# Weight buffers of two expert layers at six different starts modulo 256 bytes

## The chip, the cores and the metric

The kernel runs on one core of one Trainium2 chip. The metric is device time in microseconds of one execution, the median of several runs. Engine names are those of the profile: PE is TensorE (its weight loads are shown apart as PEld), DVE is VectorE, ACT is ScalarE, POOL is GpSimd, SP is SyncE, which here issues the DMAs.

## What is computed

Attention with a mixing matrix over the heads before and after the softmax, and behind it two expert layers (each an inner product into 2048 features, an activation and a product back to 768), all in float32:

```python
scores = scale * np.matmul(q, k.transpose(0, 1, 3, 2))        # q, k, v: (2, 12, 448, 64)
scores = np.einsum('bhij,hg->bgij', scores, w_pre)
attn = softmax over the last axis
attn = np.matmul(np.einsum('bhij,hg->bgij', attn, w_post), v)
x = attn as (896, 768)
h = x @ w_in;  x = (h * np.clip(h + 3, 0, 6) / 6) @ w_out     # w_in (768, 2048), w_out (2048, 768)
h = x @ w_in2; x = (max(h, 0) + alpha * min(h, 0)) @ w_out2
```

The weights w_in, w_out, w_in2 and w_out2 arrive as float64; the kernel makes float32 values of their bits itself.

## The kernel before, in words

**Attention, up to about 250 us.** Query rows are taken in tiles of up to 120 rows. Scores (`qk`, L192 to L200, the matmul at L197) are two matmuls per head, with qT as stationary and kT as moving operand. They are written to S, read back by `pull` (L204) so that ten rows of all twelve heads fill 120 partitions, mixed by `premix` (L220, matmul L224), put through the exponential, mixed again by `post` (L239, matmul L244, in which slices of e are stationary and wr is moving), and multiplied by v in `av` (L272, matmul L281).

**Experts.** A float32 product is made of three matmuls in the rounded type float32r, by `mm3` (L436 to L440, the matmul at L438): the high part of the weight with the high and the low part of the moving operand, then the low part of the weight with the high part of the moving operand. The stationary operand is 128 x 128 weights, 512 bytes per partition; the moving operand is 128 x 448, a whole tile of 1792 bytes per partition (xh and xl in the inner products, gh and gl in the products back). `in_layer` (L486) takes one weight block of 128 x 768 per feature block and makes 18 matmuls of it for each of the two batches; `out_layer` (L649) takes a weight block per pair of feature blocks and makes 36 of it in six accumulators. There are 64 blocks, 16 for each of the four weight matrices, and 36 matmuls for each.

**Weights.** Block i is loaded as 64-bit words (`load_w`, L332) and turned into a float32 in `wb` by `conv_magnitude` (ACT, L344), `conv_shift` and `conv_sign` (DVE, L352 and L361) and `conv_round` (POOL, L368). `conv_hi` (L373, the copy at L376) rounds it into `whi` on ACT, and `conv_lo` (L379, the subtraction at L382) puts the rest into `wlo` on POOL. In the loops this is done two blocks ahead of its use. `whi` and `wlo` have three buffers each, taken in turn, so that block i uses number i mod 3.

**Where the buffers lie.** `open_early` (L391) closes pools of the attention and opens the pool "w" in their place, on the right side of the memory, then a pool "gap" of 192 bytes (L398), then "x0" and "g0"; `open_x1` and `open_late` open the rest. The tiles of the pool "w" thus lie where kT, qT and the staging tiles of the attention lay, and their first writer waits for the last reader of those. Below, the *rest* of a tile is the remainder of its first byte's address, within a partition, by 256.

```python
hi = P["w"].tile([128, WC], R, tag="whi", bufs=3, name="whi")    # WC = 768, 3072 bytes
nc.scalar.copy(hi, b_t[i])
...
nc.tensor.matmul(p, wt[a], xt[c], start=(first and z == 0), stop=(last and z == 2))
```

Of the kernel before, what the change touches and what calls it, by code (L numbers as in the profile page):

```python
# [8 lines left out]
R = mybir.dt.float32r  # L9
# [26 lines left out]
def kernel(  # L36
# [29 lines left out]
    for b in range(B):  # L66
        for i0 in range(0, S, GP):
            n = min(GP, S - i0)
            t = len(tiles)
# [31 lines left out]
    with tc.manual_schedule():  # L101
# [201 lines left out]
        for ti in range(1, NTILE):  # L303
            lo, hi = tiles[ti - 1]["s"] - PL, tiles[ti]["s"] - PL
# [5 lines left out]
        for ti in range(NTILE - 1):  # L310
            lo = tiles[ti]["s"] + tiles[ti]["ng"] + LAG
# [4 lines left out]
        P = {}  # L316
        WC = w_in1.shape[2]
# [50 lines left out]
        def conv_round(i):  # L368
            if i < len(blocks):
                n = b_t[i].bitcast(I32)  # L370
                nc.gpsimd.tensor_tensor(n, n, st_t.pop(i)[:, :, 0].bitcast(I32), ALU.add)  # L371

        def conv_hi(i):  # L373
            if i < len(blocks):
                hi = P["w"].tile([128, WC], R, tag="whi", bufs=3, name="whi")
                nc.scalar.copy(hi, b_t[i])  # L376
                w_t[i] = [hi]

        def conv_lo(i):  # L379
            if i < len(blocks):  # L380
                lo = P["w"].tile([128, WC], R, tag="wlo", bufs=3, name="wlo")
                nc.gpsimd.tensor_tensor(lo, b_t.pop(i), w_t[i][0].bitcast(F32), ALU.subtract)  # L382
                m = KD if blocks[i][0] == "in" else 2
                w_t[i] = [x.rearrange("p (k f) -> p k f", k=m) for x in (w_t[i][0], lo)]
# [101 lines left out]
        def in_layer(i, xs, act, gs, f0):  # L486
            for f in range(f0, KF):
                conv_round(i + 2)
                load_w(i + 4)
                conv_magnitude(i + 3)  # L490
                for c in range(B):
                    p = in_chain(i, xs, c)
                    gs[f, c] = g_tile(f, c)
                    a = act(p, gs[f, c], f)
                    next(a)
                    if c == 0:
                        conv_shift(i + 3)
                        next(a)
                        conv_hi(i + 2)
                        conv_lo(i + 2)  # L500
                    else:
                        conv_sign(i + 3)
                        next(a)
                    run(a)
                w_t.pop(i)
                i += 1
            return i
# [46 lines left out]
        for i in range(NC):  # L554
            at(X + 2 + 3 * i, lambda i=i: conv_hi(i), lambda i=i: conv_lo(i))
# [78 lines left out]
        for f in range(NC):  # L634
            p = in_chain(f, x_t, 1)
            w_t.pop(f)
            if f + 3 < 5:
                conv_hi(f + 3)
                conv_lo(f + 3)
            gs[f, 1] = g_tile(f, 1)  # L640
            run(act1(p, gs[f, 1], f))
            if f + 3 < 5:
                load_w(f + 5)
                if f == 0:
                    conv_round(4)
                else:
                    conv_a(5)
# [117 lines left out]
```

## Time and profile before

| | |
|---|---|
| median of 3 runs | 710.85 us (710.15 to 712.19) |
| span of the profiled execution (the page gives no time beside it) | 710.7 us |
| PE busy, PEld busy | 693.8 us (98%), 608.7 us (86%) |
| DVE, ACT, POOL busy | 414.7, 376.5, 335.3 us |
| granted PE clock | 1.000 over the span |
| matmul records of the expert layers (L438) | six groups of 384, each 138.5 to 141.9 us busy |
| subtraction of the low part (L382), 64 times | 132.3 us, mean 2067 ns |
| copy of the high part (L376), 64 times | 53.1 us, mean 830 ns |

A matmul's own duration counts from its start to its modelled end, and matmuls overlap, so the durations of a group add up to more than the time it fills; the distance between the starts of two matmuls tells how fast they follow each other. The same holds for the weight loads, which overlap the matmul before.

### The profile page before, as it was taken

The numbers are of one execution on the slowest core, as the hardware profiler recorded it, in microseconds if no ns is written. First come the engines' busy times: TensorE is split into PE (matmuls) and PEld (weight loads), VectorE is DVE, ScalarE is ACT, GpSimd is POOL, SyncE is SP. The second block draws the span as 40 slices with busy tenths as digits, with TensorE's granted clock in tenths as the row PEclk, the third lists the DMA queues.
The fourth block names the chain that finished last, engine by engine and source line by source line (L and its number), as shares of the span: only waits on it lengthen the run. The fifth ranks groups of instructions, "written<-read, shape, count | busy, mean of one in ns | idle before, by whom it ended". The sixth has DMA issues, their size and how long they took to land.

```text
span 710.7 us, 11175 instructions
## 1 busy us (share of the span) xinstructions
PE 693.8 (98%) x4164; PEld 608.7 (86%) x4164; DVE 414.7 (58%) x790; ACT 376.5 (53%) x704; POOL 335.3 (47%) x224
## 2 busy tenths in 40 slices
PE   5899999999999999999999999999999999999998
PEld 3577777877788879998889999999999999999997
DVE  5565486456666557777774354437777778335311
ACT  4576566657776646656654453344454545433310
POOL 6331175212225244656667755444555556664630
PEclk9999999999999999999999999999999999999999
DMA  4853554346445023233234424331323243424302
GB/s 127 231 187 109 190 162 125 116 141 185 158 110 165 1 71 109 90 98 124 89 100 155 146 89 134 102 121 52 127 92 131 90 132 102 157 98 169 131 1 77
DMA packets 31875, 85.21 MB, mean 120 GB/s; under 512 B 5966, under 2 KB 21966, under 8 KB 31822
## 3 DMA queue, kind: packets, MB, share of 16 engines
q1 hardware_dynamic: 31822, 84.50, 36.6%
q8 instruction: 33, 0.54, 0.3%
q14 instruction: 20, 0.16, 0.1%
HBM read 62.47 MB, written 2.75 MB: 92 GB/s over the span
## 4 chain that ended last, share of the span: by engine, by line
PE 77%; issue 9%; POOL 7%; DVE 2%; DMA 2%; ACT 2%; SPq 1%; POOLq 0%; ACTq 0%
PE p L438 49%; PE pt L244 9%; PE mx L224 9%; PE av L281 5%; POOL wb L371 4%; PE sc L197 4%; POOL wlo L382 2%; PE sc L186 1%; DMA pull<-S 1%; DMA kst<-in_k_dram 0%; DVE nm L226 0%; DVE xl L295 0%; ACT xh L294 0%; DMA qst<-in_q_dram 0%; DVE wr L218 0%
## 5 line engine op out<-in xcount | busy, mean ns | idle before, releaser
L382 POOL TENSOR_TENSOR wlo<-wb,whi 128x768 fp32r<-128x768 f32 x64 | 132.3, 2067 | 164.7 <-ACT whi L376 164.7
L371 POOL TENSOR_TENSOR wb<-wb,wst 128x768 int32<-128x768 int32 x64 | 130.5, 2040 | 57.7 <-DVE wb L364 37.6
L438 PE MATMUL p<-xh,whi 128*128 128x448 f32 x384 | 141.9, 370 | 1.1 <-ACT xh L294 1.1
L438 PE MATMUL p<-xh,wlo 128*128 128x448 f32 x384 | 139.2, 362 | 0.6
L438 PE MATMUL p<-xl,whi 128*128 128x448 f32 x384 | 139.7, 364 | 0.0
L438 PE MATMUL p<-gl,whi 128*128 128x448 f32 x384 | 139.4, 363 | 0.0
L438 PE MATMUL p<-gh,whi 128*128 128x448 f32 x384 | 139.2, 362 | 0.0
L438 PE MATMUL p<-gh,wlo 128*128 128x448 f32 x384 | 138.5, 361 | 0.3
L356 DVE TENSOR_SCALAR wb<-wb 128x768 f32<-128x768 f32 x64 | 62.1, 970 | 90.9 <-ACT wb L348 90.9
L348 ACT ACTIVATE wb<-wst 128x768 f32<-128x768 f32 x64 | 58.1, 908 | 77.0 <-DMA wst<-in_w_out_dram 46.5
L244 PEld LDWEIGHTS pt<-wr,e 120*112 120x112 f32 x720 | 86.8, 176 | 7.5 <-issue 2.3
L234 ACT ACTIVATE e<-mx,nm 120x448 f32<-120x448 f32 (+1 forms) x90 | 57.4, 637 | 62.6 <-DVE sm L215 45.3
L244 PE MATMUL pt<-wr,e 120*112 120x120 f32 x720 | 88.5, 266 | 0.0
L224 PE MATMUL mx<-pull,wmix_pre 120*120 120x448 f32 x180 | 84.1, 549 | 3.5 <-DMA pull<-S 3.2
L226 DVE TENSOR_REDUCE nm<-mx 120x1 f32<-120x448 f32 (+1 forms) x90 | 56.0, 622 | 47.0 <-PE mx L224 47.0
L438 PEld LDWEIGHTS p<-xh,whi 128*128 128x128 f32 x384 | 72.0, 188 | 9.0 <-ACT xh L294 2.8
L438 PEld LDWEIGHTS p<-xh,wlo 128*128 128x128 f32 x384 | 71.9, 187 | 7.2 <-POOL wlo L382 2.5
L438 PEld LDWEIGHTS p<-xl,whi 128*128 128x128 f32 x384 | 72.1, 188 | 5.8 <-issue 1.1
L438 PEld LDWEIGHTS p<-gh,wlo 128*128 128x128 f32 x384 | 71.8, 187 | 6.0 <-POOL wlo L382 1.0
L438 PEld LDWEIGHTS p<-gh,whi 128*128 128x128 f32 x384 | 72.1, 188 | 5.6
L376 ACT CAST whi<-wb 128x768 fp32r<-128x768 f32 x64 | 53.1, 830 | 43.2 <-PE p L438 39.1
L197 PE MATMUL sc<-kT,qT 128*120 128x448 f32 (+1 forms) x168 | 73.8, 524 | 2.0 <-POOL kT L154 0.9
(52 smaller groups left out, 863.3 us busy)
## 6 DMA issues: line engine op xcount, KB each, us to landing
wst<-in_w_in_dram SPq DMA_DIRECT2D x32, 768.0 KB
wst<-in_w_out_dram SPq DMA_DIRECT2D x32, 768.0 KB
pull<-S SPq DMA_DIRECT2D x88, 210.0 KB
qst<-in_q_dram SPq DMA_DIRECT2D x20, 180.0 KB
kst<-in_k_dram SPq DMA_DIRECT2D x5, 672.0 KB
v<-in_v_dram SPq DMA_DIRECT2D x8, 336.0 KB
out_dram<-o SPq DMA_DIRECT2D x12, 224.0 KB
qst<-in_q_dram SPq DMA_DIRECT2D x8, 132.0 KB
```

Source lines behind the costliest of these rows:

```text
L197: nc.tensor.matmul(p[:n, :S], t[:, o, a:a + n], kT[h], start=(o == 0), stop=(o == 1))
L224: nc.tensor.matmul(m[:pn, :S], wpre[:pn, :pn], d[:pn], start=True, stop=True)
L226: nc.vector.tensor_reduce(nm[:pn], m[:pn, :S], axis=AX.X, op=ALU.max, negate=True)
L234: nc.scalar.activation(out=e[:pn], in_=m[:pn, :S], func=ACTF.Exp, bias=nm[:pn], accum_out=sm[:pn])
L244: nc.tensor.matmul(p[:, c * GP:(c + 1) * GP], e[:pn, c * JP:(c + 1) * JP], wr[:pn], start=True, stop=True,)
L281: nc.tensor.matmul(p[64 * o:64 * o + 64, a % 3, :n], v_t[T["b"], h // HC][:, h % HC, c, :], MT[ti][:, c, h, :n], start=(c == 0), stop=(c = ...
L348: nc.scalar.activation(t, s[:, :, 1].bitcast(F32), ACTF.Abs)
L356: nc.vector.tensor_scalar(t, t, W_MAX, W_MIN, ALU.min, ALU.max)
L371: nc.gpsimd.tensor_tensor(n, n, st_t.pop(i)[:, :, 0].bitcast(I32), ALU.add)
L376: nc.scalar.copy(hi, b_t[i])
L382: nc.gpsimd.tensor_tensor(lo, b_t.pop(i), w_t[i][0].bitcast(F32), ALU.subtract)
L438: nc.tensor.matmul(p, wt[a], xt[c], start=(first and z == 0), stop=(last and z == 2))
```

## The change

The pool "w" gets six tags with one buffer each in place of two tags with three. Each buffer is a little longer than the block (784 elements, the last 816), and the block starts 0, 4, 8 or 12 elements (0 to 48 bytes) into it. The starts are all multiples of 16 bytes. The six buffers together take 18944 bytes in place of 18432, 512 more, so that every tile that lies behind them keeps its rest.

```diff
@@ -370,15 +370,21 @@
                 n = b_t[i].bitcast(I32)
                 nc.gpsimd.tensor_tensor(n, n, st_t.pop(i)[:, :, 0].bitcast(I32), ALU.add)
 
+        def part(i, tag, more, starts):
+            z = i % 3
+            room = WC + 16 + (more if z == 2 else 0)
+            t = P["w"].tile([128, room], R, tag=f"{tag}{z}", bufs=1, name=tag)
+            return t[:, starts[z]:starts[z] + WC]
+
         def conv_hi(i):
             if i < len(blocks):
-                hi = P["w"].tile([128, WC], R, tag="whi", bufs=3, name="whi")
+                hi = part(i, "whi", 0, (0, 4, 8))
                 nc.scalar.copy(hi, b_t[i])
                 w_t[i] = [hi]
 
         def conv_lo(i):
             if i < len(blocks):
-                lo = P["w"].tile([128, WC], R, tag="wlo", bufs=3, name="wlo")
+                lo = part(i, "wlo", 32, (0, 0, 12))
                 nc.gpsimd.tensor_tensor(lo, b_t.pop(i), w_t[i][0].bitcast(F32), ALU.subtract)
                 m = KD if blocks[i][0] == "in" else 2
                 w_t[i] = [x.rearrange("p (k f) -> p k f", k=m) for x in (w_t[i][0], lo)]
```

In the built programs the blocks start at these rests:

| block number i mod 3 | whi before | whi now | wlo before | wlo now |
|---|---|---|---|---|
| 0 | 192 | 192 | 192 | 0 |
| 1 | 192 | 80 | 192 | 128 |
| 2 | 192 | 224 | 192 | 48 |

Slices of 128 columns lie 512 bytes apart, so a slice has its block's rest. The moving operands xh, xl, gh and gl start at rest 0 before and now. In the attention, which does not change, the stationary tiles start at other rests: the mixing matrix of L224 at 0; the four slices of e, 448 bytes apart, at 0, 192, 128 and 64; the slices of qT at all multiples of 32; v at 160, 96 and 224.

No engine's instructions change their order. The waits of four instructions on POOL do, since the buffers now lie over other old tiles. This is POOL's order at the first three low parts, before (xl is the splitting of x, wb and wst belong to the conversion):

```order
L382 TENSOR_TENSOR wlo<-wb,whi 128x768 [waits PE_49,Activation_49]
L434 TENSOR_TENSOR xl<-xT,xh 128x448 [waits Activation_49] x2
L434 TENSOR_TENSOR xl<-xT,xh 128x448 [waits DVE_49,Activation_49,Pool_49]
L382 TENSOR_TENSOR wlo<-wb,whi 128x768 [waits PE_49,Activation_49]
L434 TENSOR_TENSOR xl<-xT,xh 128x448 [waits Activation_49]
L382 TENSOR_TENSOR wlo<-wb,whi 128x768 [waits Activation_49]
```

and now:

```order
L388 TENSOR_TENSOR wlo<-wb,whi 128x768 [waits Activation_49]
L440 TENSOR_TENSOR xl<-xT,xh 128x448 [waits Activation_49] x2
L440 TENSOR_TENSOR xl<-xT,xh 128x448 [waits DVE_49,Activation_49,Pool_49]
L388 TENSOR_TENSOR wlo<-wb,whi 128x768 [waits Activation_49]
L440 TENSOR_TENSOR xl<-xT,xh 128x448 [waits Activation_49]
L388 TENSOR_TENSOR wlo<-wb,whi 128x768 [waits PE_49,Activation_49]
```

The first two subtractions no longer wait for PE, the third does. A little later stands the rounding of block 3, before:

```order
L434 TENSOR_TENSOR xl<-xT,xh 128x240 [waits DMAHW3_49,DMAHW4_49,DMAHW2_49,DMAHW5_49,DMAHW1_49,DMAHW6_49,DMAHW0_49,Activation_49]
L434 TENSOR_TENSOR xl<-xT,xh 128x240 [waits Activation_49] x4
L371 TENSOR_TENSOR wb<-wb,wst 128x768 [waits DMAHW6_49,DVE_49]
L434 TENSOR_TENSOR xl<-xT,xh 128x240 [waits Activation_49]
L382 TENSOR_TENSOR wlo<-wb,whi 128x768 [waits PE_49,Activation_49,Pool_49]
```

and now:

```order
L440 TENSOR_TENSOR xl<-xT,xh 128x240 [waits DMAHW3_49,DMAHW4_49,DMAHW2_49,DMAHW5_49,DMAHW1_49,DMAHW6_49,DMAHW0_49,Activation_49]
L440 TENSOR_TENSOR xl<-xT,xh 128x240 [waits Activation_49] x4
L371 TENSOR_TENSOR wb<-wb,wst 128x768 [waits DMAHW6_49,DVE_49,PE_49]
L440 TENSOR_TENSOR xl<-xT,xh 128x240 [waits Activation_49]
L388 TENSOR_TENSOR wlo<-wb,whi 128x768 [waits PE_49,Activation_49,Pool_49]
```

The rounding has a wait for PE more. In all of these the PE instruction waited for is a score matmul of the attention (L197).

## Rows read from the trace of the kernel before

**Rows 1.** the page: span, busy times by engine (share of the span, instructions)

```profile
span 710.7 us, 11175 instructions
...
PE 693.8 (98%) x4164; PEld 608.7 (86%) x4164; DVE 414.7 (58%) x790; ACT 376.5 (53%) x704; POOL 335.3 (47%) x224
```

**Rows 2.** the chain of waits in order of time, from 369 us: start us, us, what

```profile
369.03 338.29 PE p L438 x1690
```

**Rows 3.** windows of L438 alone: stretch, length, busy us by engine (instructions), clock, DMA

```profile
369.00:708.00 339.00, 338.27 (x1690) 316.80 (x1690) 1.00 0.32 110
```

**Rows 4.** L197, scores: ns smallest/median/largest, first and last start us

```profile
L197 PE MATMUL sc<-kT,qT x168: 358/369/722, 15.1 to 204.4; 128*120 128x448 f32 x120, 128*88 128x448 f32 x48
```

**Rows 5.** first low parts on GpSimd, timeline: start us, us, engine, line, operation

```profile
213.67 1.82 POOL L382 TENSOR_TENSOR wlo<-wb,whi 128x768 fp32r<-128x768 f32 x1
```

**Rows 6.** weight loads by line and shape: count | busy us, mean ns | idle before

```profile
L244 PEld LDWEIGHTS pt<-wr,e 120*112 120x112 f32 x704 | 84.9, 176 | 7.4 <-issue 2.3 <-ACT xh L433 0.4 <-ACT MT L257 0.2
L438 PEld LDWEIGHTS p<-xl,whi 128*128 128x128 f32 x384 | 72.1, 188 | 5.8 <-issue 1.1
...
L281 PEld LDWEIGHTS av<-MT,v 112*64 112x64 f32 x768 | 36.9, 137 | 2.1 <-ACT t L458 0.3 <-issue 0.3
L224 PEld LDWEIGHTS mx<-pull,wmix_pre 120*120 120x120 f32 x176 | 25.5, 183 | 6.3 <-POOL qT L169 2.9 <-issue 1.6 <-ACT e L234 1.3
L197 PEld LDWEIGHTS sc<-kT,qT 128*120 128x120 f32 x120 | 21.5, 183 | 25.1 <-issue 18.0 <-POOL qT L170 2.3 <-POOL kT L154 1.7
L197 PEld LDWEIGHTS sc<-kT,qT 128*88 128x88 f32 x48 | 7.6, 158 | 9.9 <-issue 9.1 <-POOL qT L170 0.4 <-POOL qT L169 0.2
```

**Rows 7.** L438 over the whole run: ns smallest/median/largest, starts

```profile
L438 PEld LDWEIGHTS p<-xl,whi x384: 186/188/192, 220.0 to 591.3; 128*128 128x128 f32 x192
```

**Rows 8.** timeline of the steady rhythm

```profile
600.15 0.36 PE L438 MATMUL p<-gh,wlo 128*128 128x448 f32 x1
...
600.34 0.36 PE L438 MATMUL p<-gh,whi 128*128 128x448 f32 x1
600.35 0.19 PEld L438 LDWEIGHTS p<-gl,whi 128*128 128x128 f32 x1
600.55 0.36 PE L438 MATMUL p<-gl,whi 128*128 128x448 f32 x1
```

**Rows 9.** timeline with loads that start late

```profile
255.23 0.36 PE L438 MATMUL p<-xh,wlo 128*128 128x448 f32 x1
...
255.25 0.19 PEld L438 LDWEIGHTS p<-xh,whi 128*128 128x128 f32 x1
255.43 0.37 PE L438 MATMUL p<-xh,whi 128*128 128x448 f32 x1
...
255.51 0.19 PEld L438 LDWEIGHTS p<-xl,whi 128*128 128x128 f32 x1
255.63 0.37 PE L438 MATMUL p<-xl,whi 128*128 128x448 f32 x1
```

**Rows 10.** L438 from 540 to 700 us

```profile
L438 PE MATMUL p<-gl,whi x180: 363/363/363, 592.1 to 699.5; 128*128 128x448 f32 x180
...
L438 PE MATMUL p<-gh,wlo x180: 360/360/360, 592.3 to 699.7; 128*128 128x448 f32 x180
```

**Rows 11.** L438 from 275 to 320 us

```profile
L438 PE MATMUL p<-xh,whi x76: 360/360/363, 274.7 to 319.7; 128*128 128x448 f32 x76
...
L438 PE MATMUL p<-xh,wlo x75: 360/363/363, 275.1 to 319.5; 128*128 128x448 f32 x75
```

**Rows 12.** tile whi: the instructions that write it, and that make wlo from it

```profile
L376 ACT CAST whi<-wb x64: 816/832/858, 212.4 to 685.6; 128x768 fp32r<-128x768 f32 x64
L382 POOL TENSOR_TENSOR wlo<-wb,whi x64: 1817/1885/2567, 213.7 to 686.5; 128x768 fp32r<-128x768 f32 x64
```

**Rows 13.** windows, all engines: stretch, length, busy us PE, PEld, DVE, ACT, POOL

```profile
540.00:700.00 160.00, 160.00 (x802) 150.00 (x801) 80.85 (x111) 60.76 (x81) 84.51 (x43) 1.00 0.32 108
```

**Rows 14.** L438 from 323 to 370 us: what ended its idle time

```profile
  POOL wlo L382: 3.5, 7
```

## The prediction

> **What bounds the kernel.** I read the page first, then the chain of waits, then the groups, timelines and windows of the expert matmuls (L438). The page is to show TensorE busy for 98% of a span of 710.7 us [rows 1]. The chain is to show what that work is in the second half: from 369.03 us to within 4 us of the end it is one piece, 338.29 us of L438 [rows 2]. Over those last 340 us nothing but the distance from one matmul to the next sets the time. No separate time stands beside the span of the profiled execution; the runs' median of 710.85 us is 0.15 above the span, and I carry the forecast on the runs' scale.
>
> The distance itself comes from the windows: 1690 matmuls in 338.27 us of busy time [rows 3], 200.2 ns each, at a granted clock of 1.00, which is the 2.4 GHz level. 448 columns at 2.4 GHz are 186.7 ns (an estimate), so 13.5 ns of each matmul is something else. There are 2304 such matmuls (64 blocks of 36), so 31.0 us of the run is at stake, and 1 ns per matmul is 2304 ns, 0.32% of the time. About 0.3%, 2.1 us, is also what a measurement of this kernel can tell from no change. The question is therefore narrow: does a weight buffer's start move the distance by 0.9 ns or more?
>
> **The change, part by part.**
>
> *Instructions.* None is added, removed or moved. The three buffers of each tag rotated by i mod 3 before and do so now. Price 0.
>
> *Waits.* Because the weight pool is 512 bytes longer, its buffers lie over other tiles of the attention. Two of GpSimd's first three low-part subtractions lose a wait for TensorE; the third, and the rounding of block 3, gain one. These are waits for readers of the old kT and qT tiles, and the last score matmul starts by 204.4 us [rows 4], while the first low part is computed from 213.7 us on [rows 5]. Old and new waits are over before they are reached, so I count 0 for both. If I read that wrongly, what is queued behind the waiting subtraction is GpSimd's splitting of x, and behind that TensorE's first expert matmuls.
>
> *Weight loads.* Five of the six buffers that the 2304 loads read start elsewhere. At rest 192 they take 188 ns [rows 6]. No row shows 128 columns at another rest, so the nearest rows must do: loads of 64 columns average 137 ns, of 88 columns 158, of 112 columns 176, of 120 columns 183 (the scores and the first mix alike), of 128 columns 188 [rows 6]. From 64 to 128 columns that is 51 ns over 64 columns, 0.8 ns a column; the line gives 156, 175 and 182 in between, and the rows lie within 2 ns of it. These loads start at very different rests: the mixing matrix at 0, e at 0, 192, 128 and 64 (slices of 448 bytes), qT at all multiples of 32 (three buffers, slices of 480 bytes). The number of columns explains the load; little is left over for the start. So I take 0. The ends come from the spread of the 128-column loads, 186 to 192 ns against 188 [rows 7]: 2 ns less or 4 ns more. If the distance followed the load one for one, that would be 2304 x 2 ns = 4.6 us less, or 2304 x 4 ns = 9.2 us more.
>
> Does the distance follow the load? In the steady rhythm a load starts within 0.01 us of the previous matmul, and the matmuls lie at 600.15, 600.34 and 600.55 [rows 8]. At 255.51 us a load starts 0.08 us after its predecessor's matmul at 255.43, and its own matmul still starts 0.20 us after that one, at 255.63 [rows 9]. A load started 0.07 us late costs nothing, so a load longer by a few ns should cost nothing either. The same rows speak to a clash of the two reads. A load at another moment of the stream meets other bytes of the moving operand, just as a load from another rest does, and the loads that start 0.02 and 0.08 us into the stream leave 0.20 us.
>
> *The moving operand.* Its tiles shift by 512 bytes or not at all, and keep rest 0. Price 0.
>
> *A trace of an address effect?* Matmuls with the low parts last 360 ns, those with the high weights and gl 363 [rows 10]. But from 275 to 320 us the 360 ns belongs to the high weights with xh, and the low weights have a median of 363 [rows 11], with the same buffers and rests. The 3 ns belong to a rhythm of three matmuls, not to a buffer.
>
> *Other engines.* ScalarE writes the high part in 816 to 858 ns, GpSimd the low part in 1.8 to 2.6 us [rows 12]. In the steady stretch neither disturbs TensorE: from 540 to 700 us, with ScalarE busy for 60.76 of 160 us and GpSimd for 84.51 [rows 13], every gl matmul takes 363 ns and every gh matmul with a low part 360, smallest as largest [rows 10]. Only from 323 to 370 us does TensorE wait for the low part, 3.5 us in 7 waits [rows 14]. If the new rests shortened GpSimd's work, at most these 3.5 us would go; lengthening each of 7 by 70 ns, the difference between smallest and median low part [rows 12], adds 0.5 us. I take 0.
>
> **A rule against the rows.** The row gives 200.2 ns a matmul. The Trainium skill, "TensorE: Matmul & The Clock Gate", section "Back-to-back issue gap", gives a gap of columns / 2.4 GHz + 2.5 ns, an estimate of 189.2 ns here, so the row disagrees by 11 ns; were this the new rests' doing to mend, the sum would be 710.9 - 25.3 = 685.6 us. The Trainium skill, "SBUF — State Buffer", section "Who interferes with whom", speaks against any effect of this change: TensorE never waits for anyone at the memory; by that the sum stays as it is, and the 13.5 ns are something that placing cannot touch.
>
> **Sum.** 0 + 0 + 0 + 0: 710.9 us.
>
> **The rivals.**
>
> *Faster: the 13.5 ns are collisions of the weight read with the moving read, and equal rests of all six buffers made the worst of it.* For it: the excess is there in every matmul, and all loads have one and the same relation (192 against 0), so the trace cannot show a better one. Against it: the late loads [rows 9] and the line through the load times [rows 6]. Price: if the two thirds of matmuls with high parts fell from 363 to the 360 ns of the best slot [rows 10], 1536 x 3 ns = 4.6 us, which gives 706.3 us. The far end is the whole excess, 31.0 us, 680 us; I see no row that supports more than a fraction of it, and a third of it would be 700.5.
>
> *Slower: some of the new rests are worse than 192.* Mechanism: one low buffer now starts at rest 0, on the moving operand's own rest, and two others (80 and 48) at odd multiples of 16 bytes; loads from these take longer or hold up the stream, and the distance follows. Place: every matmul from 369 us on, where nothing else covers it. Price: the largest load seen, 4 ns above the median [rows 7], on all 2304 is 9.2 us, 720.1 us; on half of them 4.6 us, 715.5 us. It decides from a mean of 0.9 ns per matmul. For it: 192 is the only rest whose distance is known, and a mean over six others can fall to either side. Against it: the same two sets of rows.
>
> *The change does nothing because the start is not what the reads see.* That is the forecast itself in its strictest form: same distance, 710.9 us.
>
> **How the numbers follow.** No change worth measuring, with all terms at 0: 0.48; the late loads and the load times speak for it, both from matmuls that are not exactly these. Faster: 0.28, since the excess of 31 us leaves much room and I know of no row that says what it is. Slower: 0.24, since the price per ns is the same, but there is less that a load can lose before it covers the distance. The range goes down to 703.0, beyond the 706.3 of the faster rival but short of a third of the excess, and up to 718.0, between half and all of the slower rival's 9.2 us. Outside I leave about 0.1 on either side. The likeliest case's own range is 708.8 to 713.0.
>
> **What would show it.** If I am right, the windows from 369 us on again give 200.2 ns per matmul, loads stay at 186 to 190 ns and the chain again ends in one piece of about 338 us. If the faster rival holds, the distance falls in that window, and the matmul groups with whi and wlo show shorter durations or split into values by buffer; if the slower one, the loads' median or largest grows and the 1690 matmuls take longer than 340 us. A changed distance in the window where all else is equal makes the forecast wrong; a change only before 369 us would mean that a wait or GpSimd's work did it.

## The result and the profile after

The changed kernel takes 716.12 us (median of 4 runs, 715.37 to 718.22) beside 710.89 us (710.15 to 712.19) for the kernel before: a ratio of 1.0071, 95% interval 1.0058 to 1.0083. That is slower by 5.2 us, where the forecast was no change; the time is within the range given and near the slower rival's 715.5. The traced execution of the changed kernel is the longest of its four, 718.22 us.

The page of the changed kernel, span and TensorE, which answer to [rows 1]:

```profile
span 716.4 us, 11174 instructions
...
PE 699.8 (98%) x4164; PEld 609.1 (85%) x4164; DVE 414.1 (58%) x790; ACT 376.0 (52%) x704; POOL 336.4 (47%) x224
```

The chain of waits in order of time (start, length, what), which answers to [rows 2]; the matmul's line is L444 now:

```profile
370.27 342.75 PE p L444 x1690
```

The chain reaches its last piece 1.2 us later than before (370.27 against 369.03), and the same number of matmuls, 1690, takes 4.5 us longer. Of the 1.2 us, 1.0 stands already at the first expert matmul (at 220.66 us against 219.69), before TensorE has read any of the moved buffers; in the other runs below that matmul starts between 217.4 and 219.9 us, so this part is no price of the rests. The loss is in the distance between matmuls. The windows of L444 from 369 us on, as in [rows 3] (stretch, length, busy us of PE and PEld, clock, DMA share, GB/s):

```profile
369.00:708.00 339.00, 338.97 (x1674) 313.88 (x1673) 1.00 0.32 107
```

338.97 us by 1674 is 202.5 ns a matmul in place of 200.2, at the same granted clock of 1.00. The groups of L444 from 540 to 700 us, as in [rows 10] (ns smallest/median/largest):

```profile
L444 PEld LDWEIGHTS p<-gh,whi x172: 187/188/188, 595.9 to 699.9; 128*128 128x128 f32 x172
L444 PE MATMUL p<-gh,whi x171: 362/365/369, 596.0 to 699.5; 128*128 128x448 f32 x171
...
L444 PE MATMUL p<-gl,whi x171: 362/363/370, 596.3 to 699.7; 128*128 128x448 f32 x171
L444 PEld LDWEIGHTS p<-gh,wlo x171: 187/188/189, 596.3 to 699.7; 128*128 128x128 f32 x171
L444 PE MATMUL p<-gh,wlo x171: 360/363/369, 596.5 to 699.9; 128*128 128x448 f32 x171
```

The weight loads are as long as before, 187 to 189 ns. The matmuls, which all had one value per group, now spread up to 369 and 370 ns. The next view is the timeline of the matmuls that begin four successive blocks of 36 (start, length):

```profile
377.18 0.37 PE L444 MATMUL p<-gh,whi 128*128 128x448 f32 x1
...
384.54 0.36 PE L444 MATMUL p<-gh,whi 128*128 128x448 f32 x1
...
391.83 0.37 PE L444 MATMUL p<-gh,whi 128*128 128x448 f32 x1
...
399.07 0.37 PE L444 MATMUL p<-gh,whi 128*128 128x448 f32 x1
```

and two successive ones of the kernel before:

```profile
390.35 0.36 PE L438 MATMUL p<-gh,whi 128*128 128x448 f32 x1
...
397.55 0.36 PE L438 MATMUL p<-gh,whi 128*128 128x448 f32 x1
```

Before, every block takes 7.20 us. Now the one with its parts at 192 and 0 takes 7.36, that at 80 and 128 takes 7.29, that at 224 and 48 takes 7.24, and so they repeat to the end. The three together lose 0.29 us; over 64 blocks that would be 6.1 us (an estimate). Some of that is given back early on, where TensorE waited for GpSimd's low part: the waits for it from 323 to 370 us are 1.8 us, 4 times, in place of 3.5 us, 7 times [rows 14]:

```profile
  POOL wlo L388: 1.8, 4
```

The slowest block has its high part where it always was, at rest 192, and yet from 377.18 us on all three of its products lie 203 to 206 ns apart, those with the high part too. So the rest of the buffer that a load reads does not by itself set the price of its own matmul. Three theories were put to the chip: A, what counts is how the rest changes from one load to the next; B, what counts is a weight's rest against that of the moving operand; C, what counts is the change from block to block. B later got two forms: R, the *distance* (the weight's rest less the moving operand's, modulo 256) decides, and S, the weight's own start does.

### The profile page after: what moved, and what is told of

Read it like the earlier page. It is cut to its first block, busy times and chain, and to the rows that moved or that the text cites. A ratio compares the mean times of both kernels' runs of the same rounds, so it can differ in the third digit from the quotient of the medians.

```text
span 716.4 us, 11174 instructions
## 1 busy us (share of the span) xinstructions
PE 699.8 (98%) x4164; PEld 609.1 (85%) x4164; DVE 414.1 (58%) x790; ACT 376.0 (52%) x704; POOL 336.4 (47%) x224
## 4 chain that ended last, share of the span: by engine, by line
PE 77%; issue 9%; POOL 6%; DMA 2%; DVE 2%; ACT 2%; SPq 1%; POOLq 0%; ACTq 0%
PE p L444 50%; PE pt L244 9%; PE mx L224 8%; PE av L281 5%; POOL wb L371 4%; PE sc L197 4%; POOL wlo L388 2%; DMA pull<-S 1%; PE sc L186 1%; DMA qst<-in_q_dram 1%; DMA kst<-in_k_dram 1%; DVE nm L226 0%; DVE xl L295 0%; ACT xh L294 0%; SPq L208 0%
## 5 line engine op out<-in xcount | busy, mean ns | idle before, releaser
L444 PE MATMUL p<-xh,whi 128*128 128x448 f32 x384 | 143.1, 373 | 1.1 <-ACT xh L294 1.1
L444 PE MATMUL p<-gh,whi 128*128 128x448 f32 x384 | 140.3, 365 | 0.0
L444 PE MATMUL p<-xh,wlo 128*128 128x448 f32 x384 | 140.0, 365 | 0.2
L444 PE MATMUL p<-xl,whi 128*128 128x448 f32 x384 | 140.2, 365 | 0.0
L444 PE MATMUL p<-gh,wlo 128*128 128x448 f32 x384 | 140.0, 364 | 0.2
L444 PE MATMUL p<-gl,whi 128*128 128x448 f32 x384 | 139.9, 364 | 0.0
L224 PE MATMUL mx<-pull,wmix_pre 120*120 120x448 f32 x180 | 84.0, 549 | 3.9 <-DMA pull<-S 3.2
L444 PEld LDWEIGHTS p<-xh,whi 128*128 128x128 f32 x384 | 72.0, 188 | 9.4 <-ACT xh L294 2.8
L444 PEld LDWEIGHTS p<-xl,whi 128*128 128x128 f32 x384 | 72.2, 188 | 6.9 <-issue 1.1
L444 PEld LDWEIGHTS p<-xh,wlo 128*128 128x128 f32 x384 | 72.2, 188 | 6.8 <-POOL wlo L388 1.3
L444 PEld LDWEIGHTS p<-gh,wlo 128*128 128x128 f32 x384 | 72.2, 188 | 6.6 <-POOL wlo L388 0.9
L444 PEld LDWEIGHTS p<-gl,whi 128*128 128x128 f32 x384 | 72.2, 188 | 5.6
L444 PEld LDWEIGHTS p<-gh,whi 128*128 128x128 f32 x384 | 72.0, 188 | 5.8
```

Of the source, the lines that this page charges most:

```text
L224: nc.tensor.matmul(m[:pn, :S], wpre[:pn, :pn], d[:pn], start=True, stop=True)
```

## The experiments

All experiments share one layout: six tags with buffers of 832 elements (13 times 256 bytes), so that a starting element sets the rest of each block freely, and every other tile keeps its rest unless said otherwise. The first one in full:

```diff
+        def part(i, tag, starts):
+            t = P["w"].tile([128, WC + 64], R, tag=f"{tag}{i % 3}", bufs=1, name=tag)
+            return t[:, starts[i % 3]:starts[i % 3] + WC]
...
-                hi = P["w"].tile([128, WC], R, tag="whi", bufs=3, name="whi")
+                hi = part(i, "whi", (16, 16, 16))
...
-                lo = P["w"].tile([128, WC], R, tag="wlo", bufs=3, name="wlo")
+                lo = part(i, "wlo", (16, 16, 16))
```

Below, a *triple* is the sum of three successive distances between matmul starts in the trace, for the three products of one slice; means leave out the first three triples of a block and those with a wait in them. Before, every steady triple from 380 us on is 600 ns.

**The rests undone, the rest of the change kept.** All six at 192, with starts (0, 0, 0):

> The six tags with longer buffers as in the change, the pool 1536 bytes longer than before, but all six blocks at rest 192 again: the rests undone, all the rest of the change kept. If the rests are the whole of it (theory R): 200.2 ns per matmul, no change against the kernel before, 711 us, and no run near 716. If the tags, the places or the moved waits have a share in the 5 us: 712 to 716 us.

Measured: 711.37 us (10 runs, 710.70 to 712.31) against 711.53 of the kernel before beside it, ratio 0.9999 (0.9989 to 1.0009). Windows from 369 us:

```profile
369.00:708.00 339.00, 337.70 (x1689) 316.19 (x1687) 1.00 0.33 110
```

200 ns per matmul (337.70 / 1689), and every steady triple is 600 ns. Six tags, longer buffers and other places cost nothing measurable in this layout, and the rests are what is left to explain the 5.2 us. (The pool is 1536 bytes longer than before here, in the change 512, so the change's own places and moved waits were not run by themselves.)

**All at rest 0**, starts (16, 16, 16) for both parts:

> All six weight buffers at rest 0, the moving operand's own rest, each block 0 and equal. Theory A (what counts is how far the rest changes from one load to the next): no change of rest anywhere, so 200.2 ns per matmul and 710.9 us, as before. Theory B (what counts is a buffer's rest against the moving operand's): rest 0 is the bad one, since block number 0 with its low part at 0 had the slowest triples, 613 ns in place of 600; all loads at 0 give at least 204.5 ns a matmul, 2304 x 4.3 ns more, 721 us or later. Theory C (what counts is the change from block to block): as before, 710.9 us.

Measured: 716.59 us (716.13, 716.23, 716.95 and 724.08) against 711.18, ratio 1.0106 (1.0049 to 1.0164); from 369 us, in the run of 716.23:

```profile
369.00:708.00 339.00, 339.00 (x1674) 314.50 (x1673) 1.00 0.32 108
```

202.5 ns per matmul, and steady triples of 608 ns. Equal rests do not save the time, so theory A falls, and C with it, since no block differs from another. B has the sign, but not the size: rest 0 is not as bad as the slow block of the change. One block of the trace, from 360.0 us, runs at 620 ns a triple; the run of 724.08 us has no trace.

**One pair for all blocks**, high at 192 and low at 0, starts (0, 0, 0) and (16, 16, 16):

> High parts at rest 192, low parts at rest 0, the same for all three block numbers. Theory A: every triple is like those of block number 0 in the change, 613.3 ns, 204.4 ns per matmul, so 710.9 + 2304 x 4.2 ns = 720.6 us. Theory B: the same, since the same rests stand against the moving operand. Theory C: no change from block to block, so 710.9 us.

Measured: ten runs in two groups, four from 712.48 to 713.70 and six from 718.38 to 719.52 us, against 711.18. The traced run is of the first group, and its steady triples have a mean of about 603 ns, not 613:

```profile
369.00:708.00 339.00, 338.55 (x1684) 316.24 (x1682) 1.00 0.33 110
```

No theory had this. The pair can run in more than one rhythm: in this same trace two blocks, from 344 and from 352 us, run at 613 to 614 ns a triple, and in the change two blocks of this pair, from 332 and from 354 us, have triples of about 603 ns in their steady part.

**The other pair**, high at 224 and low at 48, starts (8, 8, 8) and (28, 28, 28):

> High parts at rest 224, low parts at 48, the same for all three block numbers. In the change this block ran at 610 to 617 ns for its first two or three triples and then at 600. Theory A: after the few first triples it stays at 600, so 200.2 ns per matmul and 711 us. Theory B: 711 us too. Theory C (the first slow triples of each block come from the change of block): 711 us. If the slow triples come back at each new block though no rest changes there, some 1.0 to 2.0 us more.

Measured: 711.69 us (10 runs) against 711.18, ratio 1.0003 (0.9994 to 1.0013), triples of 600 ns in all blocks:

```profile
369.00:708.00 339.00, 338.23 (x1690) 316.92 (x1690) 1.00 0.33 110
```

As every theory had it; the slow first triples do not come back when no rest changes. Two unequal rests can be as good as the kernel before.

**Equal within a block, different by block**, 192, 80 and 224, starts (0, 36, 8) for both parts:

> High and low part of a block at the same rest, 192, 80 and 224 for the three block numbers. Theory A: only the one load in 36 at which the block changes sees another rest; a few slow triples behind it, at most 711 to 713 us. Theory B: blocks at 80 and 224 keep the price that they had in the change for their high parts, 2304 x 2/3 x about 1.5 ns = 2.3 us, 713.2 us. Theory C: the whole loss of the change, 716 us.

Measured: 717.51 us against 711.18, ratio 1.0090 (1.0073 to 1.0106). The timeline of the first matmuls of successive blocks, at 80, 224, 192 and again 80:

```profile
404.58 0.37 PE L442 MATMUL p<-gh,whi 128*128 128x448 f32 x1
...
411.91 0.37 PE L442 MATMUL p<-gh,whi 128*128 128x448 f32 x1
...
419.34 0.37 PE L442 MATMUL p<-gh,whi 128*128 128x448 f32 x1
...
426.55 0.37 PE L442 MATMUL p<-gh,whi 128*128 128x448 f32 x1
```

7.33 us at 80, 7.43 at 224, 7.21 at 192, in the products back as in the inner products. But for one block (at 224, from 344.9 us, 612 ns a triple), each rest has a time of its own, to the end of its block; only 0.01 us per block at 192 is left for the change of block. The price of 224 alone (620 ns a triple, 6.7 ns a matmul) is far above the 1.5 ns that theory B had read for it from the change, where 224 stood with 48.

**Weights against the moving operand.** Weights at 0, 144 and 32, starts (16, 52, 24) for both parts, and x moved to rest 64 by a smaller gap in front of its pool; g stays at 0 (but for the four tiles of pool g0):

```diff
-            pool(ctx, "gap", bufs=1, side="right").tile([128, 48], F32, name="gap")
+            pool(ctx, "gap", bufs=1, side="right").tile([128, 32], F32, name="gap")
```

> Weights at rest 0, 144 and 32 by block number, high and low part alike, and the moving operand of the inner products (x) shifted to rest 64, while that of the products back (g) stays at 0. Less x's rest, the weights then stand at 192, 80 and 224 in the inner products. Theory R (the distance from the moving operand's rest decides): in the inner products steady triples of 600, 610 and 620 ns, as at 192, 80 and 224 in the run by block; in the products back 608 ns for block number 0, as with all at 0, and two values not known. Theory S (the weight's own start decides, whatever the moving operand does): 608 ns for block number 0 in both, and the same value in both kinds of product for the other two.

Measured: 716.80 us in a single run. The same weight buffer, at rest 0, in a product back and in an inner product; the first matmul of its block and of the next block, in the timeline:

```profile
396.29 0.37 PE L442 MATMUL p<-gh,whi 128*128 128x448 f32 x1
...
403.59 0.37 PE L442 MATMUL p<-gh,whi 128*128 128x448 f32 x1
...
484.28 0.37 PE L442 MATMUL p<-xh,whi 128*128 128x448 f32 x1
...
491.49 0.37 PE L442 MATMUL p<-xh,whi 128*128 128x448 f32 x1
```

7.30 us where g starts at 0 (distance 0), 7.21 where x starts at 64 (distance 192). The blocks of the inner products then take what the run by block took at the same distances: steady triples of 601, 610 and 618 ns, and blocks of 7.21, 7.32 and 7.43 us. One of them, from 343.9 us at distance 224, runs at 600 all the same. That inner products and products back differ in themselves is ruled out by the run by block, where both kinds take the same time at each rest. So here it is the place of the moving operand that differs. Theory S falls; theory R holds, though one distance can have more than one time.

**Scans.** With R, each run shows six distances, three in the inner products and three in the products back. Starts (20, 40, 56) with a gap of 40 elements, and (28, 44, 60) with a gap of 56:

> Weights at rest 16, 96 and 160 by block number, x at rest 32, g at 0: distances 240, 64 and 128 in the inner products and 16, 96 and 160 in the products back. A look at six distances not seen yet. Theory R: triples between 600 and 620 ns, differing between inner products and products back of the same block number; if the time were a smooth sum over collisions, values near 192 (160) would be low and those near 224 and 80 high. If 600 ns is a floor that no placing passes, none is under 600; if the 13 ns beyond 448 columns are all collisions, some distance gives down to 560.

> Weights at rest 48, 112 and 176 by block number, x at rest 224, g at 0: distances 80, 144 and 208 in the inner products and 48, 112 and 176 in the products back. Theory R: 610 ns at distance 80, as in the run by block, the rest between 600 and 620. Theory S: each block number has one value in both kinds of product. Floor as in the scan before: none under 600 if the 13 ns are not collisions.

Measured: 716.63 and 718.41 us, a single run each. Mean steady triples by distance, with those of the runs by block and of the moved x (1 ns either way hangs on which triples at the seams of blocks are counted):

| distance | ns | distance | ns | distance | ns | distance | ns |
|---|---|---|---|---|---|---|---|
| 0 | 608 | 64 | 607 | 128 | 611 | 192 | 600 to 601 |
| 16 | 620 | 80 | 610 | 144 | 608 to 610 | 208 | 613 |
| 32 | 613 | 96 | 602 | 160 | 616 | 224 | 618 to 620 |
| 48 | 608 | 112 | 612 | 176 | 610 | 240 | 610 |

Distance 80 has its 610 again, at another weight rest and another x rest. It is no smooth curve, and no distance has a mean under 600. In these runs 192, where the kernel before stood with all buffers, and 96 are the best, 16 and 224 the worst.

**Starts between multiples of 16 bytes**, at 200, 104 and 4, starts (2, 42, 17), gap of 40 elements (x at 32):

> Weights at rest 200, 104 and 4 by block number, so distances 200, 104 and 4 in the products back; x at rest 32, so 168, 72 and 228 in the inner products: starts that are no multiple of 16 bytes. Theory R with 600 ns as its floor: between 600 and 622, none lower. If only whole steps of 16 bytes count: the values of 192 (600), 96 (600) and 0 (608) in the products back. If a finer placing avoids more of the collisions: under 600.

Measured: 716.91 us in a single run. Products back: 601 at 200, 610 at 104, 613 at 4; inner products: 619 at 168, 610 at 72, 605 at 228. None is under 600, and 104 is not like 96, nor 4 like 0: finer steps seem to count, but win nothing here.

**The best and the worst distance in all buffers**, starts (40, 40, 40) and (8, 8, 8) for both parts:

> All six weight buffers at rest 96, the other distance at which the scan saw triples of 600 ns. Theory R: 200.2 ns per matmul and no change against the kernel before, 711 us. If it is not the distance alone but something that only 192 has: 605 ns or more, 715 us.

> All six weight buffers at rest 224, the distance with the slowest steady triples seen, 620 ns. Theory R: 206.7 ns per matmul, 2304 x 6.5 ns = 15 us more than before, 726 us, though high and low part lie at equal rests. If equal rests helped at all: under 716 us.

Measured at 96: 710.91, 711.83, 724.24 and 724.31 us, in two groups again, with a granted clock of 0.995 to 0.997 in both. The traced run is the first; its groups from 390 us on, and in one block near 355 us:

```profile
L442 PE MATMUL p<-gh,whi x325: 362/362/363, 389.9 to 699.5; 128*128 128x448 f32 x163
```

```profile
L442 PE MATMUL p<-xl,whi x10: 367/367/368, 352.7 to 358.3; 128*128 128x448 f32 x10
```

Measured at 224: 723.05 us (722.48 to 723.50) against 711.42, ratio 1.0165 (1.0148 to 1.0182). Its groups from 280 to 305 us, and from 540 to 590 us:

```profile
L442 PE MATMUL p<-xh,whi x42: 362/362/362, 280.0 to 304.6; 128*128 128x448 f32 x42
L442 PEld LDWEIGHTS p<-xl,whi x42: 187/188/188, 280.0 to 304.6; 128*128 128x128 f32 x42
```

```profile
L442 PE MATMUL p<-xh,whi x81: 369/369/369, 539.8 to 589.4; 128*128 128x448 f32 x81
...
L442 PEld LDWEIGHTS p<-xh,whi x81: 188/188/188, 540.2 to 589.8; 128*128 128x128 f32 x81
```

Both distances know two rhythms, of 600 and of 620 ns a triple, in one and the same execution: 362 ns a matmul in the one, 367 to 369 in the other. With 224 the rhythm of 600 holds until a single weight load starts late:

```profile
311.92 2.43 POOL L386 TENSOR_TENSOR wlo<-wb,whi 128x768 fp32r<-128x768 f32 x1 [2.96 <-ACT whi L380]
...
314.36 0.37 PE L442 MATMUL p<-xl,whi 128*128 128x448 f32 x1
...
314.40 0.19 PEld L442 LDWEIGHTS p<-xh,wlo 128*128 128x128 f32 x1
314.56 0.37 PE L442 MATMUL p<-xh,wlo 128*128 128x448 f32 x1
```

The low part is ready at 314.35 us, and the first load that reads it starts 0.045 us after the matmul before it in place of 0.002. Its own matmul still follows in 0.20 us (314.56), but the next triples are 608, 615 and then 620 ns throughout. With 96 the load at the same place starts 0.022 us late, the next three distances are 202, 204 and 201 ns, and 600 comes back. After that the rhythm at 224 changes several times where TensorE waits for low parts (one block, from 329 us, has 613), and after the last of these waits, near 367 us, 620 holds to the end; with 96 a block near 355 us runs at 620, and after the next wait 600 holds to the end. 15 us were expected of 224 and 11.6 came, since 620 did not hold from the start. That the two runs of 724 us at 96 stayed at 620 would fit, but no trace of them was taken, so it is not shown.

**Shorter loads.** All rests at 192 as before; the second and the third product use 64 of the 128 weight columns, so half of the low-order correction is left out:

```diff
+                n = 64 if z and not (last and z == 2) else 128
                 nc.tensor.matmul(
-                    p, wt[a], xt[c], start=(first and z == 0), stop=(last and z == 2)
+                    p[:n], wt[a][:, :n], xt[c], start=(first and z == 0), stop=(last and z == 2)
                 )
```

> All rests as before (192 against 0). Of the three products of each weight slice, the second and the third load and multiply 64 of the 128 weight columns (but for the last of a chain), so half of the low-order correction is left out. Theory L (the 13.5 ns beyond 448 columns are the moving read giving way to the weight read, in proportion to what is loaded): two loads of three half as long, triples of 600 - 2 x 6.7 = 587 ns, and about 10 us less, 701 us. Theory F (13.5 ns are a fixed cost of each matmul, whatever it loads): 600 ns and 711 us.

Measured: 715.27 us in a single run, against 711.42. From 369 us:

```profile
369.00:708.00 339.00, 338.80 (x1682) 258.40 (x1682) 1.00 0.32 108
```

The loads' busy time falls from 316.80 us [rows 3] to 258.40 and the matmuls lie no closer: 201.4 ns. Theory L falls in the form given: the 13.5 ns beyond the 448 columns do not shrink in proportion to the load. F is not settled either, since the triples are no longer 600 throughout but wander (means of 603 in the products back and 605 in the inner products). Changing the length of some loads costs time just as changing their starts does.

## Why the prediction missed, and what of it held

**What bounds the kernel** held: the distance between expert matmuls from 369 us on sets the time, 1 ns of it is 2.3 us, and 0.9 ns was the point from which it would show. Measured were 2.3 ns (202.5 against 200.2).

**Waits, conversion, other engines, the shift of the tiles**: 0, and 0 was measured with all six at 192 again (0.9999), where the shift was 1536 bytes and not 512.

**"The number of columns explains the load; little is left over for the start"** held for the load and was the wrong question. From 380 us on, full loads take 186 to 192 ns at every distance traced, and all of them 188 in the run at 224, where matmuls follow each other in 206.7 ns. The distance does not follow the load's time. So the term "weight loads", taken at 0, was the wrong one in the sum: 2.3 ns by 2304 matmuls are 5.3 us, beside 5.2 measured.

**"Does the distance follow the load?" is the step that failed.** From loads that started 0.02 and 0.08 us late [rows 9] I read that meeting other bytes of the moving operand costs nothing, because the distance stayed at 0.20 us. Those rows are rounded to 10 ns, and the effect asked for was 1 to 6 ns. In the trace's starts, which are in whole ns, those two distances are 204 and 203 ns, where the steady ones are 197, 202 and 201, with a mean of 200. Two distances prove little, but 3 or 4 ns is the size that was asked for; taken at 3 ns, the same rows would have bounded the change at about 7 us. The run at 224 answers the step directly: there one load, 0.045 us late, leaves its own matmul's distance at 0.20 us and yet turns the rhythm from 200.0 to 206.7 ns. With all rests equal no row of the kernel before could show the effect in the steady stretch; that should have weighed more than two rows that could not resolve it.

**"The 3 ns belong to a rhythm of three matmuls, not to a buffer"** held, and was the better trail: a rhythm that can sit differently is what the runs found.

**The slower rival** had the sign, the place and nearly the size, 715.5 us against 716.1. That its number is so near is luck: it priced loads that take 4 ns longer on half of the matmuls, and the loads did not get longer. Its other half (the stream is held up) fits the wider spacing, and its bad rest was not the worst: distance 0 costs 608 ns a triple, distances 16 and 224 cost up to 620. The time lies inside the range because room was left for this rival, not through the sum. (13.5 ns by 2304 is 31.1 us, not 31.0, and five rests were new, not six; neither changes anything.) **The faster rival** supposed that equal rests of 192 were the worst placing. They were among the best: 192 has 600, and no mean under 600 was seen with full loads at 16 multiples of 16 bytes and 6 others, so the excess of 13.5 ns was not touched. **The rule that TensorE never waits for anyone at the memory** (the Trainium skill, "SBUF — State Buffer", section "Who interferes with whom") agreed with the trace as to other engines: with ScalarE and GpSimd busy for 60.76 and 84.51 of 160 us [rows 13], every gl matmul takes 363 ns [rows 10]. What the prediction drew from it, that placing this kernel's weights has no effect, the measurements contradict: TensorE's own two operands, placed otherwise, move the distance from 200.0 to 206.7 ns.

**What stays open.** That the distance between the two starts counts, and not the weight's own start, is shown by moving x. It does not settle the time alone, since 96, 224 and the pair of 192 and 0 each have two rhythms. That the two reads meet in the same part of the memory is the plain reading of it, but it was only argued: no run shows the memory itself. Why a steady matmul takes 200.0 ns and not 186.7, and which rhythm a wait leads into, was not settled. No version faster than the kernel before was found; it stands at the best distance seen, and in the rhythm of 600 where it was traced.

## What to carry to other kernels

Where matmuls follow each other without a gap and each brings its own weights, the start of the weights less the start of the moving operand, modulo 256 bytes, can be worth up to 3% of that stretch (620 against 600 ns a triple); buffers of a multiple of 256 bytes keep one distance for all. One run per distance is not enough to choose by: 96 looked as good as 192 in its trace, and half of its runs took 13 us more. Take several runs, and keep a distance only when none of them falls out. Spreading buffers over many rests mixes good distances with bad ones, and needs a reason in the trace first. And an effect of a few ns per instruction is not to be ruled out from rows rounded to 10 ns: take a mean over hundreds of instructions, or starts in whole ns.

## What the hardware showed beyond that

One placing can have two steady rhythms. At distances 96 and 224 the same program runs at 600 or at 620 ns a triple, and a wait of TensorE, or a single load that starts 0.045 us late, can switch between them; at 96 the runs fall into 710.9 to 711.8 and 724.2 to 724.3 us, with the pair 192 and 0 into 712.5 to 713.7 and 718.4 to 719.5, and at 0 one of four runs took 724.1 where the others took 716.1 to 717.0. A few runs of such a kernel can agree by chance. The kernel before, at 192, ranged from 710.05 to 712.95 us over all its runs beside these experiments, with no second group.
